# Gates and ids in a tensor of their own, two batches' parks on SyncE, eight copies on VectorE, and w2 behind w_out in a step

## The chip, the cores and the metric

The kernel runs on one core of a Trainium2 chip, so the execution has one slowest core and one clock. The metric is the device time of one execution in microseconds (us), the median of several runs. Five engines work at once and each runs its own instructions in order: TensorE (PE, matmuls; PEld is its weight loads), VectorE (DVE), ScalarE (ACT), GpSimd (POOL) and SyncE (SP, which here only issues DMAs). DMAs are issued from SP, from ACT and, where they are indirect, from POOL; a DMA instruction that has to wait holds whatever stands behind it on the engine that issues it.

## What is computed

Three layers in a row on 8 x 3072 tokens of 256 channels. First a long convolution along the sequence, written as an FFT. Then a mixture of 8 experts with one expert for each token, in which an expert takes at most 768 tokens *of the whole 24576*, in order; all others get a row of zeros. Last a dense pair of layers with a softplus between.

```python
# x: (8, 3072, 256)
X = np.fft.rfft(x, axis=1); y = np.fft.irfft(X * (filt_r + 1j * filt_i)[None], n=3072, axis=1)
x = y.reshape(24576, 256)
logits = x @ w_gate                         # (N, 8); e = argmax, gate = softmax at e
# token i goes to slot counts[e] of expert e as long as counts[e] < 768, in order of i
h = np.maximum(np.einsum('ecd,edf->ecf', disp, w1), 0.0)     # F = 1024
y = np.einsum('ecf,efd->ecd', h, w2)
out[i] = gate[i] * y[e, slot]               # 0 where the token has no slot
h2 = out @ w_in                             # (N, 2048)
return (np.maximum(h2, 0) + np.log1p(np.exp(-np.abs(h2)))) @ w_out
```

## The kernel before

**The convolution** is a DFT by two matmul stages each way (3072 = 96 x 32). Only the first three batches (called static, `STATIC = 3`) are convolved ahead, since they can fill all 6144 slots; more is computed only if a flag says that slots are empty. Of a batch, `tr1` transforms the input, `load_i` fetches a tile `it` of the half-way result from a DRAM tensor `mid`, `s2` multiplies it with `m2s` (L235) and with the filter (tile `z`), `s3` goes back (tile `e`), and then, for each of eight groups g of 384 rows and each half h of the channels, `tr2` transposes (L262) and copies to a tile `j` (L265), `s4` multiplies with `m4s` (L299) and copies to the tile `yt` (L300), and `park` (L365) writes `yt` to a DRAM tensor `parked` of the batch. `yt` has three buffers, and the zero tile `pf` with which `prefill` (L382) clears the dispatch tensor `disp` in 16 DMAs is one of them until the last of these DMAs has read it.

**The routing.** `gsum`, `gturn` and five steps of `gate` give each row its expert, its gate and its slot. `marks` writes gate and token id as two more columns into `parked` (256 floats of row and these 2, so a row has 258), in four DMAs of 8-byte pieces on SP (L372), and the slots into `slots` (L373). `send` loads the slots as an index (`ixt`, L390); `fetch` loads 384 parked rows with gate and id into a tile `lt` (L394; three buffers); `scatter` writes them to `disp` by indirect DMAs from POOL (L398), 24 for a batch. After the last scatter of batch 1 the first unit's rows `xd` are loaded (L535).

**Experts and dense layers** run over 16 units of 384 slots, two for each expert. `tr_x` turns `xd` to `xh`/`xl` (L555, L556), `w1` (L566) and `w2` (L583, tile `py`, taken to `yh`/`yl` by L589 and L590) are the expert; `wi` (L598, tile `pi`) the first dense layer, `sp_act` on ACT and `sp_sum` on DVE (L501, tile `g`) the softplus, `wo` (L621, tile `po`) the second. fp32 precision comes from products of high and low parts, so a weight `ws` is split into `w1h`, `w1l`, `w2h`, `w2l` by ACT and POOL (L412, L413); the dense weights come in as `wst` (L452) and are split by `convert` into `wih`, `wil`, `woh`, `wol` on DVE, ACT and POOL.

**What sets the order.** The program is emitted by hand: `ev(t, order, fn)` puts a piece of work at a step t with a rank, and the pieces are issued by step, then rank. The steps count from c0 = -72; below "step 20" is c0 + 20, and the steps from 0 on (72 after c0) are those in which `wi` and `wo` run. The batches begin at steps 0, 17 and 29. `marks` of a batch is 22 steps on, `send` 23; the prefills stand at steps 5 to 20, the four `wst` loads of `x_done` at 22, the scatters of batch 0 at 26 to 37 (two a step) and of batch 1 at 43 to 50 (three a step). The tail of the last static batch is at 44 to 52: two `tr2`, two `s4` and one park in each. From step 0 on the ranks say `w2`, `wi`, softplus, `wo`, and `w1` behind; `w2` is there in every other step, `w1` in the others.

DMAs from SP and ACT take turns, in the order in which they are written, on eight completion semaphores. A DMA therefore waits until the one eight places earlier has landed, from whichever of the two queues that was.

## Time and profile before

| what | us |
|---|---|
| median of 3 runs | 1128.05 |
| lowest and highest of them | 1123.34, 1129.77 |
| the profiled execution | 1124.01 |
| its span in the trace | 1122.1 |
| PE busy in the span | 1040.6 (93%) |
| ACT busy | 804.6 (72%) |
| POOL busy | 598.1 (53%) |
| DVE busy | 478.8 (43%) |

How to read it: the profiled execution is one execution and lies 4.04 us below the median and 0.67 us above the lowest run; 1.91 us of it lie outside the span. PE is the busiest engine over the whole, but the share is a mean over stages. The convolution lasts until about 262 us of the span and the way into the dense layers until about 365 us; behind that comes one long even stage. In the rows below, "a <- b" behind an engine says what it waited for: b is the releaser. In a timeline, the bracket says how long the engine was idle before the row, and on what.

### The profile page before, as it was taken

Reading aid. Unit: us, or ns where it says so; the run is one execution under the profiler, and the core shown is the slowest. Engines: PE = TensorE matmul, PEld = TensorE weight load, DVE = VectorE, ACT = ScalarE, POOL = GpSimd, SP = SyncE. Lnnn points to the kernel's source line nnn. Section 1 sums busy time; section 2 is a strip of 40 time slices with the busy share of each in tenths; the row PEclk is TensorE's granted clock in tenths of the full one; section 3 lists DMA queues with packets and bytes.
Section 4 is the critical chain, followed back from the end, with each engine's and each line's share of the span. In section 5 each row is a group of like instructions: output and inputs, shape, how many; then the busy total and the mean of one; then the engine's idle time right before and its main releaser. Section 6 shows DMA issues by size and latency. Waiting matters only on the chain.

```text
span 1122.1 us, 18349 instructions
## 1 busy us (share of the span) xinstructions
PE 1040.6 (93%) x6608; PEld 963.6 (86%) x6608; DVE 478.8 (43%) x929; ACT 804.6 (72%) x1690; POOL 598.1 (53%) x566
## 2 busy tenths in 40 slices
PE   9999788666778999999999999999999999999996
PEld 7655566336778999999999999999999999999996
DVE  3526699336867472323232333233333333232221
ACT  3554445455778888877887878888788787887885
POOL 0410284544555756677656564655646565554554
PEclk9999999977999999999999999999999999999999
DMA  9997787776542317633333333242211212100000
GB/s 305 319 323 207 191 247 164 210 239 148 159 130 83 91 48 254 217 109 129 113 114 113 109 113 114 91 144 81 76 53 55 60 52 62 53 11 15 15 15 18
DMA packets 111416, 141.69 MB, mean 126 GB/s; under 512 B 24367, under 2 KB 82988, under 8 KB 111313
## 3 DMA queue, kind: packets, MB, share of 16 engines
q1 hardware_dynamic: 87632, 105.73, 31.1%
q10 hardware_dynamic: 17920, 22.02, 6.8%
q0 software_dynamic: 5760, 12.65, 3.2%
q8 instruction: 54, 0.88, 0.3%
q14 instruction: 50, 0.40, 0.1%
HBM read 80.38 MB, written 63.15 MB: 128 GB/s over the span
## 4 chain that ended last, share of the span: by engine, by line
PE 71%; DMA 8%; DVE 6%; issue 6%; ACT 3%; POOL 3%; SPq 1%; POOLq 0%; ACTq 0%; DVEq 0%
PE pi L598 22%; PE po L621 22%; PE py L583 9%; PE pw L566 9%; DMA it<-mid 2%; DMA mid<-s 2%; PE p L235 2%; POOL disp L398 1%; PE p L199 1%; PE p L219 1%; PE p L299 1%; POOL gl L413 1%; PE p L254 1%; DVE wr L475 1%; DMA xt<-in_x_dram 1%
## 5 line engine op out<-in xcount | busy, mean ns | idle before, releaser
L501 DVE SCALAR_TENSOR_TENSOR g<-pi,ln 128x384 f32<-128x384 f32 x256 | 142.8, 558 | 498.5 <-ACT ln L496 455.5
L413 POOL TENSOR_TENSOR gl<-g,gh 128x384 fp32r<-128x384 f32 x256 | 260.5, 1021 | 114.4 <-ACT gh L412 76.3
L621 PE MATMUL po<-woh,gh 128*128 128x256 f32 x768 | 214.9, 280 | 3.7 <-DVE ot L628 3.7
L621 PE MATMUL po<-woh,gl 128*128 128x256 f32 x768 | 215.6, 281 | 0.8 <-POOL gl L413 0.8
L621 PE MATMUL po<-wol,gh 128*128 128x256 f32 x768 | 215.8, 281 | 0.0
L493 ACT ACTIVATE ab<-pi 128x384 f32<-128x384 f32 x256 | 125.0, 488 | 114.4 <-PE pi L598 103.3
L598 PE MATMUL pi<-yh,wih 128*128 128x384 f32 x512 | 173.5, 339 | 6.4 <-DVE g L501 6.4
L598 PE MATMUL pi<-yl,wih 128*128 128x384 f32 x512 | 172.4, 337 | 0.0
L598 PE MATMUL pi<-yh,wil 128*128 128x384 f32 x512 | 172.2, 336 | 0.0
L413 POOL TENSOR_TENSOR w1l<-ws,w1h 128x512 fp32r<-128x512 f32 x64 | 83.4, 1303 | 148.9 <-ACT w1h L412 145.4
L621 PEld LDWEIGHTS po<-woh,gh 128*128 128x128 f32 x768 | 144.3, 188 | 4.5 <-DVE ot L628 2.6
L621 PEld LDWEIGHTS po<-woh,gl 128*128 128x128 f32 x768 | 144.8, 188 | 1.0 <-POOL gl L413 1.0
L621 PEld LDWEIGHTS po<-wol,gh 128*128 128x128 f32 x768 | 144.2, 188 | 0.0
L494 ACT ACTIVATE ab<-ab 128x384 f32<-128x384 f32 (+1 forms) x257 | 134.9, 525 | 8.2
L496 ACT ACTIVATE ln<-ab 128x384 f32<-128x384 f32 (+1 forms) x257 | 134.8, 524 | 8.1
L412 ACT CAST gh<-g 128x384 fp32r<-128x384 f32 x256 | 129.6, 506 | 0.3 <-DVE g L501 0.3
L413 POOL TENSOR_TENSOR w2l<-ws,w2h 128x512 fp32r<-128x512 f32 x64 | 83.3, 1301 | 84.6 <-ACT w2h L412 82.7
L598 PEld LDWEIGHTS pi<-yh,wih 128*128 128x128 f32 x512 | 96.5, 188 | 8.5 <-DVE g L501 8.4
L243 POOL TENSOR_TENSOR z<-z,t 128x512 f32<-128x512 f32 x24 | 31.0, 1292 | 126.1 <-DVE t L242 94.9
L598 PEld LDWEIGHTS pi<-yl,wih 128*128 128x128 f32 x512 | 96.4, 188 | 0.0
L598 PEld LDWEIGHTS pi<-yh,wil 128*128 128x128 f32 x512 | 96.1, 188 | 0.0
L583 PE MATMUL py<-hh,w2h 128*128 128x384 f32 x256 | 89.6, 350 | 6.4 <-DVE yl L590 6.4
(132 smaller groups left out, 2000.7 us busy)
## 6 DMA issues: line engine op xcount, KB each, us to landing
ws<-in_w_dram SPq DMA_DIRECT2D x128, 256.0 KB
out_dram<-cs SPq DMA_DIRECT2D x48, 512.0 KB
lt<-parked SPq DMA_DIRECT2D x24, 387.0 KB
xt<-in_x_dram SPq DMA_DIRECT2D x24, 384.0 KB
parked<-yt ACTq DMA_DIRECT2D x24, 384.0 KB
disp<-pf SPq DMA_DIRECT2D x16, 387.0 KB
xd<-disp SPq DMA_DIRECT2D x48, 129.0 KB
mid<-s ACTq DMA_DIRECT2D x16, 384.0 KB
```

What stands on the lines that cost most here:

```text
L235: nc.tensor.matmul(ps[:, i], lhsT=self.m2s[:, p0 + i], rhs=it[:, i], start=True, stop=True)
L243: (nc.vector if b > 0 and k % 2 else nc.gpsimd).tensor_tensor(out=z, in0=z, in1=t2, op=ALU.add)
L412: nc.scalar.copy(dst_hi, src)
L413: nc.gpsimd.tensor_tensor(out=dst_lo, in0=src, in1=dst_hi.bitcast(F32), op=ALU.subtract)
L493: nc.scalar.activation(out=ab[:, :n], in_=h, func=ACTF.Abs)
L494: nc.scalar.activation(out=ab[:, :n], in_=ab[:, :n], func=ACTF.Exp, scale=-1.0)
L496: nc.scalar.activation(out=ln[:, :n], in_=ab[:, :n], func=ACTF.Ln, bias=1.0)
L501: nc.vector.scalar_tensor_tensor(out=g[:, :n], in0=h, scalar=0.0, in1=ln[:, :n], op0=ALU.max, op1=ALU.add)
L566: nc.tensor.matmul(ps, lhsT=a[:, k, fs], rhs=b[:, k], start=(n == 0), stop=(n == 5))
L583: nc.tensor.matmul(self.py[d], lhsT=a[:, j % 2, ds], rhs=b, start=(j == 0 and n == 0), stop=(j == 7 and n == 2))
L598: nc.tensor.matmul(self.pi, lhsT=a[i][:, k], rhs=b[:, k], start=(n == 0), stop=(n == 5))
L621: nc.tensor.matmul(self.po[t], lhsT=a[:, ts], rhs=b[:, i], start=(i == 0 and n == 0), stop=(i == KI - 1 and n == 2))
```

## The change

It does five things. **Tensors:** `parked` keeps 256 columns, and gates and ids go to a new DRAM tensor `marked` of two columns. A park then writes 96 contiguous pieces of 4 KB where it wrote 384 of 1 KB; `marks` is one DMA instead of four; `load_rows` is two DMAs, one for the rows and one for gate and id, whose pieces in the tile are 8 bytes. **Queues:** the parks of batches 0 and 1 are issued by SP, those of batch 2 stay on ACT. **Copies:** of the last batch, the copies to `j` with h = 0, eight in all, go to DVE. **Steps:** the prefills come three steps later, `marks` one, `send` with its two fetches two, the scatters of batch 0 one. **Ranks:** `w2` comes behind `wi`, the softplus and `wo` in a step. Behind the change the lines of the file move by one or two: L365 is L367, L394 is L395 and L396, L452 is L454, L583 is L585, L598 is L600.

```diff
@@ -112,7 +112,8 @@
     const = ctx.enter_context(tc.tile_pool(name="const", bufs=1))
     dram = ctx.enter_context(tc.tile_pool(name="dram", bufs=1, space=DRAM))
     disp = dram.tile([nslot, D + 2], F32, name="disp")
-    parked = [dram.tile([S, D + 2], F32, name=f"parked{b}") for b in range(STATIC)]
+    parked = [dram.tile([S, D], F32, name=f"parked{b}") for b in range(STATIC)]
+    marked = [dram.tile([S, 2], F32, name=f"marked{b}") for b in range(STATIC)]
     slots = [dram.tile([S], I32, name=f"slots{b}") for b in range(STATIC)]
     mid = [dram.tile([N1 * N2, D], F32, name=f"mid{b}") for b in range(1, STATIC)]
     ltp = ctx.enter_context(tc.tile_pool(name="lt", bufs=3))
@@ -262,7 +263,7 @@
                 nc.tensor.transpose(ps[:, i], self.e[b][:, h, :, 4 * g + i], ident)
             pv = ps.rearrange("p a c -> p (a c)")
             self.jt[b, h, g] = self.jp.tile([N1, 512], F32, name="j", tag="j")
-            nc.scalar.copy(self.jt[b, h, g], pv)
+            (nc.vector.tensor_copy if b == STATIC - 1 and h == 0 else nc.scalar.copy)(self.jt[b, h, g], pv)
 
         def gsum(self, b):
 
@@ -293,11 +294,12 @@
         def s4(self, b, h, g):
             cs = slice(h * 128, h * 128 + 128)
             if h == 0:
-                self.yt[b, g] = self.yp.tile([N1, 4, D + 2], F32, name="yt", tag="yt")
+                yt = self.yp.tile([N1, 4 * (D + 2)], F32, name="yt", tag="yt")
+                self.yt[b, g] = yt[:, 0:4 * D]
             jt = self.jt.pop((b, h, g))
             ps = pso.tile([N1, 4, 128], F32, name="p6", tag="o")
             nc.tensor.matmul(ps.rearrange("p a c -> p (a c)"), lhsT=self.m4s, rhs=jt, start=True, stop=True)
-            nc.scalar.copy(self.yt[b, g][:, :, cs], ps)
+            nc.scalar.copy(self.yt[b, g].rearrange("p (a c) -> p a c", c=D)[:, :, cs], ps)
 
         def gate(self, b, late):
 
@@ -361,20 +363,19 @@
 
         def park(self, b, g):
 
-            rows = parked[b].rearrange("(g n a) c -> n g a c", n=N1, a=4)[:, g, :, 0:D]
-            nc.scalar.dma_start(rows, self.yt[b, g][:, :, 0:D])
+            queue = nc.scalar if b == STATIC - 1 else nc.sync
+            queue.dma_start(parked[b].rearrange("(g n a) c -> g n (a c)", n=N1, a=4)[g], self.yt[b, g])
 
         def marks(self, b):
 
             ga, ix = self.route[b]
-            rows = parked[b].rearrange("(g n a) c -> n g a c", n=N1, a=4)
-            for a in range(4):
-                nc.sync.dma_start(rows[:, :, a, D:D + 2], ga.rearrange("n (g a) o -> n g a o", a=4)[:, :, a])
+            nc.sync.dma_start(marked[b].rearrange("(g n a) o -> n g (a o)", n=N1, a=4),
+                              ga.rearrange("n (g a) o -> n g (a o)", a=4))
             nc.sync.dma_start(slots[b].rearrange("(g n a) -> n g a", n=N1, a=4), ix.rearrange("n (g a) -> n g a", a=4))
 
         def prefill(self):
 
-            pf = self.yp.tile([N1, 4, D + 2], F32, name="pf", tag="yt")
+            pf = self.yp.tile([N1, 4 * (D + 2)], F32, name="pf", tag="yt").rearrange("p (r c) -> p r c", c=D + 2)
             nc.gpsimd.memset(pf, 0.0)
             nc.gpsimd.memset(pf.bitcast(I32)[:, :, D + 1:D + 2], OOB)
             dv = disp.rearrange("(a p r) c -> a p r c", p=N1, r=4)
@@ -391,7 +392,8 @@
 
     def load_rows(b, g):
         rows[b, g] = ltp.tile([128, 3, D + 2], F32, name="lt", tag="lt")
-        nc.sync.dma_start(rows[b, g], parked[b].rearrange("(g p t) c -> g p t c", p=128, t=3)[g])
+        nc.sync.dma_start(rows[b, g][:, :, 0:D], parked[b].rearrange("(g p t) c -> g p t c", p=128, t=3)[g])
+        nc.sync.dma_start(rows[b, g][:, :, D:D + 2], marked[b].rearrange("(g p t) o -> g p t o", p=128, t=3)[g])
 
     def scatter_rows(b, g, t, group):
         n = hi if group == "late" else nslot
@@ -735,7 +737,7 @@
                 fn(*args)
 
         units = [Unit(e, r + e * UNIT) for r in [hi, *range(0, hi, region)] for e in range(E)]
-        W2, WI, SP, WO, SUM, W1, TAKE, TR, AHEAD = range(9)
+        WI, SP, WO, W2, SUM, W1, TAKE, TR, AHEAD = range(9)
         T1, T2, S2, GG, S4, GATE, S3, X1, ON = range(-9, 0)
 
 
@@ -844,20 +846,20 @@
                 ev(t + 1, S4, cv.s4, b, h, g)
                 if h:
                     ev(t + 1, ON, park, b, g)
-            ev(s + 22, ON, cv.marks, b)
+            ev(s + 23, ON, cv.marks, b)
             if not last:
-                ev(s + 23, ON, send, b, "lead")
+                ev(s + 25, ON, send, b, "lead")
                 for _ in range(2):
-                    ev(s + 23, ON, fetch)
+                    ev(s + 25, ON, fetch)
         for g in range(8):
             ev(c0 + 5 + g, X1, cv.x1_out, 1, g)
             ev(c0 + 5 + g, ON, cv.load_x, 2, g)
             ev(c0 + 13 + g, X1, cv.x1_out, 2, g)
         for i in range(nslot // (4 * N1)):
-            ev(c0 + 5 + i, ON, next, fills)
-        for t in range(26, 51):
-            if t < 38 or t > 42:
-                ev(c0 + t, ON, scatter, 2 if t < 38 else 3)
+            ev(c0 + 8 + i, ON, next, fills)
+        for t in range(27, 51):
+            if t < 39 or t > 42:
+                ev(c0 + t, ON, scatter, 2 if t < 39 else 3)
         ev(c0 + 22, ON, x_done)
         for t in range(c0 + 23, -24):
             ev(t, AHEAD - 0.5, convert, t < c0 + 45 and (t - c0) % 3 == 2)
```

On SP, this is the place where batch 0's marks stood, before: the marks and the slots, then the four `wst` loads of `x_done`, the index, and the first loads of rows. (`parked_61` and `slots_64` are those of batch 0.)

```order
L382 DMA disp<-pf 96x1032 x9
L372 DMA parked_61<-ga 96x8x2 x4
L373 DMA slots_64<-ix 96x8x4
L452 DMA wst<-in_win_dram 128x2x128 x4
L390 DMA ixt<-slots_64 128x8x3
L394 DMA lt<-parked_61 128x774 x3
L452 DMA wst<-in_win_dram 128x2x128
L394 DMA lt<-parked_61 128x774 x2
```

After, the parks of batch 0 stand between the prefills, and the `wst` loads ahead of the marks:

```order
L367 DMA parked_61<-yt 96x1024
L383 DMA disp<-pf 96x1032 x2
L454 DMA wst<-in_win_dram 128x2x128 x4
L367 DMA parked_61<-yt 96x1024
L372 DMA marked_64<-ga 96x8x8
L374 DMA slots_67<-ix 96x8x4
L383 DMA disp<-pf 96x1032
L367 DMA parked_61<-yt 96x1024
L391 DMA ixt<-slots_67 128x8x3
L395 DMA lt<-parked_61 128x3x256
L396 DMA lt<-marked_64 128x3x2
L395 DMA lt<-parked_61 128x3x256
```

The four `wst` loads moved from behind the marks to before them, and six parks now stand ahead of the index load, one of them behind the marks.

On ACT, this is the tail of the last batch, before, from the second half of step 44 to the split of the first expert weight (`parked_63` is batch 2, `parked_62` batch 1):

```order
L365 DMA parked_62<-yt 384x1x256
L365 DMA parked_63<-yt 384x1x256
L480 ACTIVATE whb<-wtop,ebias 128x256
L481 ACTIVATE wrf<-wrf 128x256
L300 COPY yt<-p_2019 96x4x128
L300 COPY yt<-p_2022 96x4x128
L265 COPY j<-p_2025 96x512
L265 COPY j<-p_2032 96x512
L314 ACTIVATE ex<-dl 96x256
L365 DMA parked_63<-yt 384x1x256
L300 COPY yt<-p_2111 96x4x128
```

After, from the same place:

```order
L367 DMA parked_63<-yt 96x1024
L482 ACTIVATE whb<-wtop,ebias 128x256
L483 ACTIVATE wrf<-wrf 128x256
L302 COPY yt<-p_2029 96x4x128
L302 COPY yt<-p_2032 96x4x128
L266 COPY j<-p_2042 96x512
L316 ACTIVATE ex<-dl 96x256
L367 DMA parked_63<-yt 96x1024
L302 COPY yt<-p_2122 96x4x128
L302 COPY yt<-p_2125 96x4x128
L266 COPY j<-p_2135 96x512
L367 DMA parked_63<-yt 96x1024
```

One park is gone from ACT (batch 1's last), one copy to `j` of each pair is gone, and the parks of batch 2 keep their places.

On PE, this is the beginning of step 0, before: `w2` of the third unit's first piece and then `wi` of the first unit:

```order
L583 MATMUL py<-hh,w2h 128x384
L583 MATMUL py<-hl,w2h 128x384
L583 MATMUL py<-hh,w2l 128x384
L583 MATMUL py<-hh,w2h 128x384
L583 MATMUL py<-hl,w2h 128x384
L583 MATMUL py<-hh,w2l 128x384
L598 MATMUL pi<-yh,wih_1023 128x384
L598 MATMUL pi<-yl,wih_1023 128x384
L598 MATMUL pi<-yh,wil_1031 128x384
L598 MATMUL pi<-yh,wih_1023 128x384
L598 MATMUL pi<-yl,wih_1023 128x384
L598 MATMUL pi<-yh,wil_1031 128x384
```

After, at the same place:

```order
L600 MATMUL pi<-yh,wih_1020 128x384
L600 MATMUL pi<-yl,wih_1020 128x384
L600 MATMUL pi<-yh,wil_1028 128x384
L600 MATMUL pi<-yh,wih_1020 128x384
L600 MATMUL pi<-yl,wih_1020 128x384
L600 MATMUL pi<-yh,wil_1028 128x384
L585 MATMUL py<-hh,w2h 128x384
L585 MATMUL py<-hl,w2h 128x384
L585 MATMUL py<-hh,w2l 128x384
L585 MATMUL py<-hh,w2h 128x384
L585 MATMUL py<-hl,w2h 128x384
L585 MATMUL py<-hh,w2l 128x384
```

The six matmuls to `pi` moved ahead of the six to `py`; in the following steps `wi` therefore stands alternately behind a `w2` and behind a `w1`, where before the two stood together behind `wi` of every second step.

## Rows read from the trace of the kernel before

**Rows 1.** Stretches: length, busy us (instructions) of each engine, granted clock, DMA share, GB/s.

```profile
0.00:89.00 89.00, 82.49 (x470) 58.10 (x471) 34.19 (x54) 42.57 (x73) 16.43 (x18) 1.00 0.99 314
89.00:136.00 47.00, 39.05 (x178) 25.58 (x177) 32.07 (x58) 20.59 (x39) 6.37 (x5) 0.93 0.72 188
136.00:200.00 64.00, 54.51 (x338) 40.40 (x340) 60.20 (x107) 34.09 (x68) 39.42 (x38) 1.00 0.79 205
200.00:262.30 62.30, 36.84 (x156) 18.77 (x156) 18.06 (x44) 27.13 (x55) 30.99 (x31) 0.79 0.75 205
262.30:315.00 52.70, 41.34 (x220) 38.84 (x220) 48.41 (x102) 37.17 (x89) 31.16 (x29) 0.95 0.58 174
315.00:365.00 50.00, 44.31 (x266) 42.23 (x267) 34.63 (x71) 41.85 (x98) 27.64 (x28) 0.97 0.33 93
365.00:1122.10 757.10, 742.07 (x4990) 739.67 (x4989) 251.25 (x495) 601.20 (x1271) 446.14 (x419) 1.00 0.26 86
```

**Rows 2.** What PE waited for, 100 to 136 us: us in total, times, longest.

```profile
PE p L235 <- DMA it<-mid: 6.6, 3, 3.5
```

**Rows 3.** The chain that ended last, 105 to 132 us: start, us, what.

```profile
105.55 0.69 DVE z L239
...
114.87 7.76 DMA wst<-in_win_dram
122.66 8.65 DMA it<-mid
```

**Rows 4.** Timeline of SP, DMA issues in order: start, us, engine, line.

```profile
66.87 15.63 SPq L382 DMA_DIRECT2D disp<-pf  x9
111.55 2.06 SPq L372 DMA_DIRECT2D parked<-ga  x4
```

**Rows 5.** Copies and parks in the whole trace: ns shortest/median/longest, first and last start.

```profile
L365 ACTq DMA_DIRECT2D parked<-yt x24: 557/558/1890, 83.6 to 261.2; - x24
...
L265 ACT COPY j<-p x48: 580/584/615, 76.2 to 248.1; 96x512 f32<-96x512 f32 x48
```

**Rows 6.** What PE waited for, 200 to 290 us, as in Rows 2.

```profile
PE p L299 <- ACT j L265: 8.0, 4, 6.1
PE p L299 <- DVE v L317: 6.4, 1, 6.4
PE pt L555 <- ACT xd L547: 6.0, 2, 4.8
PE pw L566 <- ACT xh L556: 5.1, 1, 5.1
```

**Rows 7.** Timeline of ACT in the last tail; bracket: idle before, and on what.

```profile
218.25 1.24 ACTq L365 DMA_DIRECT2D parked<-yt  x2
...
230.46 0.59 ACTq L365 DMA_DIRECT2D parked<-yt  x1
231.15 1.07 ACT L300 COPY yt<-p 96x512 f32<-96x512 f32 x2 [8.57 <-DMA ws<-in_w_dram]
...
238.94 0.62 ACT L412 CAST w1h<-ws 128x512 fp32r<-128x512 f32 x1
```

**Rows 8.** The chain again, 196 to 261 us.

```profile
196.13 6.76 DMA lt<-parked
...
248.79 2.55 DMA disp<-lt,ixt
...
253.92 7.18 DMA parked<-ga
```

**Rows 9.** What PE waited for, 290 to 380 us, as in Rows 2.

```profile
PE py L583 <- DVE yl L590: 6.4, 2, 3.9
PE pi L598 <- DVE g L501: 5.4, 6, 1.5
```

**Rows 10.** Scatters in the whole trace (as in Rows 5), and what their tile made wait.

```profile
L398 POOL DMA_INDIRECT disp<-lt,ixt x72: 967/992/1447, 136.3 to 548.9; - x72
...
  DMA lt<-parked: 8.6, 1
```

## The prediction

> **What bounds the kernel now.** I read the stretches first, then what TensorE waited for in each, then the chain, then the timelines of the engines that the chain names. The stretches [rows 1] fall into two kinds. From 365 us on TensorE is busy for 742.07 of 757.1 us; nothing in this change makes its matmuls fewer, so at most a few us are to be had there. Ahead of 365 us it is idle for 66.5 us of 365 (the lengths less the busy times of the first six rows), and 25.5 of these lie in 200 to 262.3, where the granted clock is 0.79 as well; 8.0 lie in 89 to 136. In 136 to 200 and in 262.3 to 315 VectorE is the busy one (60.20 of 64, 48.41 of 52.7), in 315 to 365 ScalarE (41.85 of 50). So a saving counts where TensorE waits on something that is neither of these.
>
> Two places are of that kind. **The first** is at 111 us: the waits of TensorE are 6.6 us in three pieces on tiles fetched from DRAM [rows 2], and the chain [rows 3] and SP's timeline [rows 4] say why: the marks of batch 0 go out at 111.55, behind the routing's last VectorE work, the weight loads stand behind them on SP and take 7.76 us, and only when the load's semaphore is free can the next `it` load go, which takes 8.65 more. SP is done with the prefills at 82.50 (66.87 + 15.63) and issues nothing until 111.55 [rows 4]: 29 us behind one wait. **The second** is the last tail. TensorE waits 8.0 on copies `j`, 6.4 on VectorE's `v`, 6.0 on `xd` and 5.1 on `xh` [rows 6], 25.5 us in all. ScalarE's rows [rows 7] show that it is held by its own DMAs: two parks go out only at 218.25, one at 230.46, behind which ScalarE was idle 8.57 us on an expert weight load. The chain [rows 8] then goes through the last scatter (248.79) and the marks of batch 2 (253.92, 7.18 us), which the last park waits for on ScalarE with `xh` behind it.
>
> **The early part: marks, loads, parks on SP.** Removed: SP's hold ahead of the weight loads. In the order after, the four `wst` loads stand before the marks, with one park and two prefills just ahead. The `it` loads then no longer depend on marks. Of the 6.6 us I expect 5.0 back, and about 1 us more of a smaller wait earlier as the prefills leave the stretch whose DMA share is 0.99: **6 us**. The upper bound is 8.0, all of the idle time in 89 to 136 [rows 1]. The lower bound is 2: the weight loads now start behind transfers of 384 KB, and one such round trip is as long as the `it` load's, 8.65 us, so most of the wait may come back. Moving 16 parks from ScalarE frees 16 x 0.558 = 8.9 us of its queue [rows 5], but ScalarE is busy 34.09 of 64 in 136 to 200, with VectorE full there; I cost that at nothing either way. SP has room, except for what the slower rival below says. A park of 96 pieces in place of 384 moves the same bytes; I take no gain from it, and if the DMA share of 0.72 to 0.79 falls, it helps loads that are already counted. Batch 0's scatters are a step later and end well before those of batch 1 begin: nothing.
>
> By the Trainium skill, page "Trainium Kernel Development and Optimization", section Key Constraints, DMAs of SP, ScalarE and GpSimd share the same 16 engines, and issuing from several queues only saves issue time. That rule alone would make the sixteen parks worth at most the 8.9 us above; the rows show a second effect, since what holds ScalarE for 8.57 us is the wait before an issue and no issue.
>
> **The last tail.** Eight `j` copies leave ScalarE: 8 x 0.584 = 4.7 us [rows 5] of work that lies one per step between a pair of transposes and its matmul. No VectorE copy of this shape is in the trace; the nearest, `z` of 128x512 from the same kind of source, takes 0.69 us [rows 3], so 8 x 0.69 = 5.5 us on an engine busy 18.06 of 62.3. The two copies of a pair then run beside each other. What the ScalarE queue waits for moves as well. By the semaphores that the order gives each DMA, the parks of batch 2 now wait as follows: the first on an early weight load (no hold), the next on the fourth pair of row loads, which follows the sixth scatter, the third on the fifth, the fourth on the fourth expert weight load, and the last on nothing but its copies. With scatters and loads where they are now, the first goes out by about 213 in place of 218.25, the second near 220 (rows landed at 202.9 [rows 8], six scatters of about 1.3 with what lies between them to near 211, where one alone is 0.99 [rows 10]; the landing of a scatter, 2.55, and a load of 6.76 [rows 8]) in place of 230.46, the fourth near 230, and so `w1h`, at 238.94 now [rows 7], at 230 to 234: 5 to 9 us. The scatters that stand behind its low part on GpSimd, the `xd` loads and TensorE's first expert matmul follow. On top, the last park no longer waits for the marks (7.18 us landing, of which `xh` and TensorE lose 5.1 [rows 6, 8]). Both lie on the one chain, 5 and 5: **10 us**. Lower bound 4: the first half is taken back by the loads' landing, and part of the last 5.1 goes to `xd` or a weight split that is late next. Upper bound 13: 9 and 4 at full clock instead of 0.79. What follows in 262.3 to 315 is bound by VectorE's splits, in order and behind the same work, so I let it shift as a whole.
>
> **w2 behind w_out.** In step 0 `py` must wait until the former `py` is taken: 6.4 us over two waits, the longest 3.9 [rows 9]. In the order after, `wi` of a unit whose input is long there runs in that wait; six matmuls, at 742.07 us for 4990 [rows 1], fill 0.9 us of it. Its softplus starts earlier by that wait, and `wi` comes evenly afterwards, against waits of 5.4 us on `g`; ScalarE's 41.85 of 50 lets only some of that go. I take **2 us**, with bounds of -2 (the copies `yh` now stand behind three softplus operations on ScalarE) and 5. Behind 365 us the 15 us that TensorE isn't busy are spread thin: 0.
>
> **The sum.** 6 + 10 + 2 = 18 us from the profiled 1124.01: 1106.0 on its basis. The median lies 4.04 above it and the lowest run 0.67 below, so the basis of the timed runs is 0 to 4 higher; I take 2 and say **1108**. The bounds: 2 + 4 - 2 = 4 gives 1120 and 8 + 13 + 5 = 26 gives 1098; with 0 to 4 for the basis, 1098 to 1124.
>
> **Rivals.** *(a) The small loads become the clock.* Each row load now has a twin of 8-byte pieces, 24 more DMAs. The nearest row for such pieces is the marks' landing, 7.18; the load of rows is 6.76 [rows 8], so beside it the twin costs 0 to 0.4 us, but up to 7 more for each turn of three buffers if the two land one after the other. Two parks wait for such a pair. Then `w1h` stays near 237, the tail gains 4 instead of 10, and the sum is 12 less 2 for batch 1's later start: 10, 1116. For it: two parks do wait on row loads; against it: of 72 scatters one waited for rows, the first of batch 1 [rows 10].
> By the Trainium skill, page "DMA: Bandwidth & Descriptors", section Specifications, transfers below 512 bytes don't run at line rate and are read, changed and written. By that rule the twins are the dear part of this change, and (a) would be the likelier; the rows of the same small pieces, which land in about the time of the 387 KB load, speak against more than that.
>
> *(b) Everything goes and the clock stays up.* All waits of rows 2, 6 and 9 fall to their bounds and 200 to 262.3 runs nearer to clock 1: 26 us, 1100 or a little less.
>
> *(c) Given back.* The two places open, but VectorE, full in 136 to 200 and 262.3 to 315, is behind the same work and lets nothing of the early part through, and the tail's gain is waited for at the splits: 18 becomes 4 or less, 1122 to 1126, within 0.5%.
>
> *(d) Slower: the ring of `yt`.* It has three buffers, and with the prefills three steps later one of these is `pf` until step 23; so ScalarE's copies of a group wait until the park two groups back has landed. These parks now stand on SP behind prefills, each 1.7 us of SP in a row of nine [rows 4]. Two groups are 3.25 steps, about 16 us (all parks, steps 16 to 52, go out from 83.6 to 261.2 [rows 5], 4.9 us a step). A landing is 7 to 9 us [rows 3, 8], so it decides once a park waits over 7 to 9 us on SP. If it does, three groups before step 23 lose a round trip of 8.65 each, 26, and the early 6 is gone: 26 lost, 12 saved behind it, 1140. Against it: the order has a park behind one or two prefills at most.
>
> **How the numbers follow.** The forecast 0.55 (1101 to 1114), (a) 0.15, (b) 0.08, (c) 0.12, (d) 0.10. Half a percent, about what a measurement of this kernel can tell, is 5.6 us: faster is below 1122.4, slower above 1133.7. Faster: the forecast, (a) and (b), 0.78; same: (c) and a little of (a) and (d), 0.14; slower 0.08. The range leaves out (d), the far end of (b) and that of (c): 1097 to 1124.
>
> **What would show it.** Right: no wait of TensorE on `it` over 2 us between 100 and 136; SP issues weight loads before the marks; no park on ScalarE later than about 232 until the last; `xh` without a wait on marks; `pi` runs inside the wait on `py`. Wrong: ScalarE's `yt` copies waiting for `parked` between 85 and 115 (d); GpSimd waiting for `lt` more than once between 196 and 225 (a); the stretch to 315 as long as before although 200 to 262 is shorter (c). If ScalarE still waits for a weight load in the tail, my reading of which DMA each park waits for is wrong.

## The result, and the profile after

The changed kernel takes 1114.67 us, median of 8 runs (1111.69 to 1117.72), against 1123.46 of the kernel before in 8 runs (1121.35 to 1129.77). The medians differ by 8.8 us; the ratio, which compares all runs of both, is 0.9914, with an interval of 0.989 to 0.9938: 0.86%, or 9.7 us, faster. The forecast was 1108, 16 us below the 1124 of the profiled execution; the measured time lies in its range, and a little over half of the gain came. Its profile has a span of 1112.5 us, 9.6 less than before. Where the 9.6 lie is not where the prediction put them.

The stretches of the changed kernel, with the columns and borders of [rows 1]:

```profile
89.00:136.00 47.00, 43.17 (x227) 30.42 (x225) 41.29 (x71) 25.87 (x50) 12.86 (x11) 1.00 0.94 277
...
200.00:262.30 62.30, 46.18 (x195) 31.34 (x193) 42.97 (x93) 34.99 (x78) 38.08 (x37) 0.86 0.78 234
...
365.00:1112.50 747.50, 727.49 (x4838) 718.02 (x4837) 242.37 (x475) 591.60 (x1228) 429.50 (x402) 1.00 0.26 85
```

Fixed borders mix what moved with what shrank: 200 to 262.3 has 46.18 us of TensorE where it had 36.84 and a granted clock of 0.86 in place of 0.79, but it no longer holds the same work. Four events that stand in both programs cut the span by work instead: the marks of batch 1 on SP, the first expert matmul, the first copy of `ot`, and the last.

| start, us | before | after | earlier by |
|---|---|---|---|
| marks of batch 1 (SP) | 186.70 | 178.56 | 8.1 |
| first expert matmul, to `pw` (PE) | 262.32 | 239.53 | 22.8 |
| first copy `ot` (DVE) | 384.94 | 361.21 | 23.7 |
| last group of copies `ot` | 1111.97 | 1102.31 | 9.7 |

The front gained 23.7 us and the even stage behind it gave 14.1 back. TensorE's waits in the even stage, of before and then of after (as in [rows 2]: us in total, times, longest):

```profile
PE po L621 <- DVE ot L628: 3.7, 3, 2.4
PE pi L598 <- DVE g L501: 1.0, 1, 1.0
PE po L621 <- POOL gl L413: 0.8, 1, 0.8
```

```profile
PE po L623 <- ACT ab L495: 6.6, 12, 0.5
PE po L623 <- DVE ot L630: 2.7, 4, 1.2
PE pi L600 <- DVE g L503: 1.2, 1, 1.2
```

Twelve waits of 0.5 us are new, about one for each unit. The copies `ot` show the pace: in ten of the fifteen intervals between units they came 51.1 us apart before, and come 52.3 to 52.4 apart now. One unit of before, and one of after (columns of [rows 1]):

```profile
646.38:697.49 51.11, 51.11 (x344) 51.05 (x343) 16.36 (x36) 41.07 (x87) 29.12 (x28) 1.00 0.33 109
```

```profile
627.08:679.45 52.37, 51.82 (x343) 51.14 (x342) 16.48 (x35) 41.91 (x87) 29.26 (x28) 1.00 0.33 111
```

Before, TensorE is busy without a gap; after, a unit takes 1.26 us more, of which 0.55 show as idle time. The place is at the beginning of a unit, where `wo` needs the buffers of `po` back. VectorE there in the changed kernel, and TensorE (timelines; the bracket is idle time before, and its releaser):

```profile
626.60 0.56 DVE L573 SCALAR_TENSOR_TENSOR hl<-pw,hh 128x384 fp32r<-128x384 f32 x1 [0.36 <-ACT hh L572]
627.08 1.08 DVE L630 COPY ot<-po 128x256 f32<-128x256 f32 x3
```

```profile
626.76 0.34 PE L600 MATMUL pi<-yh,wil 128*128 128x384 f32 x1
627.64 0.35 PE L623 MATMUL po<-woh,gh 128*128 128x256 f32 x1 [0.55 <-ACT ab L495]
```

The first matmul to `po` starts 0.88 us after the last to `pi`; it can start when the first `ot` is copied out of its buffer, and the copies stand on VectorE behind `hl`, the split of `w1`'s result, which waits for ScalarE's `hh` (idle 0.36 us on it in the row above) and so for `w1` itself. The releaser's name in TensorE's row, `ab`, is the event that came last by the profile, not the one waited for: its row starts at 627.13 and lasts 0.49, so it ends within 0.12 us of the first of the three copies. A run below tells the two apart. Between two units' `wo` there stood `w1`, `w2` and `wi` before; now `w1` and `wi` do.

In the front, the waits that answer to [rows 2] and [rows 6], 100 to 136 us and 200 to 290:

```profile
PE p L236 <- DMA it<-mid: 1.7, 2, 1.3
```

```profile
PE p L301 <- DVE j L266: 6.2, 5, 4.7
PE pt L557 <- ACT xd L549: 4.0, 4, 1.9
PE p L301 <- ACT j L266: 3.2, 2, 1.8
...
PE pw L568 <- ACT xh L558: 0.7, 1, 0.7
```

6.6 became 1.7, and the 5.1 on `xh` became 0.7. Of the 8.0 on ScalarE's copies `j` 3.2 are left, with 6.2 on VectorE's beside them; the 6.4 on `v` are gone, and the 6.0 on `xd` are 4.0. (The second window has fixed borders, so it doesn't hold the same work.) ScalarE's parks and the first split in the last tail (answering to [rows 7]):

```profile
213.64 0.31 ACTq L367 DMA_DIRECT2D parked<-yt  x1
...
218.66 0.31 ACTq L367 DMA_DIRECT2D parked<-yt  x1
219.01 0.62 ACT L414 CAST w1h<-ws 128x512 fp32r<-128x512 f32 x1 [3.17 <-DMA ws<-in_w_dram]
...
238.65 0.31 ACTq L367 DMA_DIRECT2D parked<-yt  x1
```

Of the chain, the parts that answer to [rows 8]:

```profile
187.35 4.38 DMA lt<-marked
...
208.09 5.47 DMA lt<-parked
```

The split `w1h` starts at 219.01, 19.9 us earlier than before, and the last park, at 238.65, waits for no marks. Last, the first step of the dense layers (answering to [rows 9]):

```profile
PE pi L600 <- DVE g L503: 5.1, 4, 2.6
PE py L585 <- DVE yl L592: 2.9, 1, 2.9
```

### The profile page after: what moved, and what is told of

Same layout as the page of the kernel before. It is cut to its first block, busy times and chain, and to the rows that moved or that the text cites. A ratio compares the mean times of both kernels' runs of the same rounds, so it can differ in the third digit from the quotient of the medians.

```text
span 1112.5 us, 18383 instructions
## 1 busy us (share of the span) xinstructions
PE 1048.5 (94%) x6608; PEld 966.5 (87%) x6608; DVE 486.3 (44%) x937; ACT 810.7 (73%) x1682; POOL 599.8 (54%) x566
## 4 chain that ended last, share of the span: by engine, by line
PE 72%; DVE 10%; DMA 6%; ACT 5%; issue 4%; POOL 2%; ACTq 1%; SPq 0%; POOLq 0%; DVEq 0%
PE pi L600 22%; PE po L623 22%; PE py L585 10%; PE pw L568 9%; PE p L220 2%; PE p L200 1%; PE p L236 1%; DMA disp<-lt,ixt 1%; ACT ab L495 1%; DVE wr L477 1%; POOL gl L415 1%; DVE whb L485 1%; DVE wrf L479 1%; DVE t L241 1%; DVE t L243 1%
## 5 line engine op out<-in xcount | busy, mean ns | idle before, releaser
L600 PE MATMUL pi<-yh,wih 128*128 128x384 f32 x512 | 176.2, 344 | 6.3 <-DVE g L503 6.3
L600 PE MATMUL pi<-yh,wil 128*128 128x384 f32 x512 | 173.2, 338 | 0.0
L600 PE MATMUL pi<-yl,wih 128*128 128x384 f32 x512 | 172.6, 337 | 0.0
L623 PEld LDWEIGHTS po<-woh,gh 128*128 128x128 f32 x768 | 145.0, 189 | 14.6 <-ACT ab L495 12.8
L600 PEld LDWEIGHTS pi<-yh,wih 128*128 128x128 f32 x512 | 96.6, 189 | 11.4 <-DVE g L503 10.4
L572 ACT ACTIVATE hh<-pw 128x384 fp32r<-128x384 f32 x128 | 62.6, 489 | 56.1 <-PE pw L568 56.1
L600 PEld LDWEIGHTS pi<-yl,wih 128*128 128x128 f32 x512 | 96.6, 189 | 0.0
L600 PEld LDWEIGHTS pi<-yh,wil 128*128 128x128 f32 x512 | 96.3, 188 | 0.0
L585 PE MATMUL py<-hh,w2h 128*128 128x384 f32 x256 | 87.9, 343 | 5.5 <-DVE yl L592 5.5
```

The costliest lines, as they stand in the source:

```text
L572: nc.scalar.activation(out=hh, in_=ps, func=ACTF.Relu)
L585: nc.tensor.matmul(self.py[d], lhsT=a[:, j % 2, ds], rhs=b, start=(j == 0 and n == 0), stop=(j == 7 and n == 2))
L600: nc.tensor.matmul(self.pi, lhsT=a[i][:, k], rhs=b[:, k], start=(n == 0), stop=(n == 5))
L623: nc.tensor.matmul(self.po[t], lhsT=a[:, ts], rhs=b[:, i], start=(i == 0 and n == 0), stop=(i == KI - 1 and n == 2))
```

## The experiments

Each run has its ratio to the kernel before on the same chip; that is what is compared, since the chips' own medians of before went from 1123 to 1129. The trace of each gives the four events of the table above. The last four rows belong to the runs at the end of this section.

| kernel | ratio (95% interval) | median, us | marks, batch 1 | first `pw` | first `ot` | last `ot` | unit |
|---|---|---|---|---|---|---|---|
| the changed kernel | 0.9914 (0.989 to 0.9938) | 1114.67 | 178.56 | 239.53 | 361.21 | 1102.31 | 52.4 |
| old ranks | 0.9769 (0.9733 to 0.9804) | 1103.5 | 177.43 | 241.73 | 365.34 | 1093.24 | 51.1 |
| ranks alone | 1.011 (1.0068 to 1.0151) | 1141.75 | 191.08 | 265.65 | 386.89 | 1129.89 | 52.3 |
| take first | 0.9792 (0.9753 to 0.9831) | 1107.49 | 178.12 | 240.86 | 363.15 | 1097.07 | 51.6 |
| old ranks, no copies on VectorE | 0.9753 (0.9715 to 0.9791) | 1101.94 | 178.33 | 238.46 | 362.75 | 1089.76 | 51.1 |
| old ranks, parks on ScalarE | 0.9892 (0.9852 to 0.9931) | 1117.05 | 185.95 | 248.41 | 372.12 | 1099.86 | 51.1 |
| old ranks, marks in the rows | 0.9868 (0.9828 to 0.9909) | 1114.84 | 183.37 | 253.35 | 376.37 | 1103.47 | 51.1 |
| old ranks, old steps | 0.9746 (0.9693 to 0.9799) | 1100.89 | 177.82 | 241.31 | 364.67 | 1092.45 | 51.1 |
| the tensor alone | 0.9899 (0.9859 to 0.994) | 1116.62 | 184.09 | 252.08 | 376.11 | 1103.15 | 51.1 |
| old ranks, pieces of 1 KB | 0.9851 (0.9818 to 0.9885) | 1105.2 | 177.77 | 243.17 | 365.78 | 1092.85 | 51.1 |
| old ranks, again | 0.9789 (0.9764 to 0.9813) | 1106.05 | 179.17 | 242.96 | 367.29 | 1094.28 | 51.1 |
| pieces of 1 KB, again | 0.9809 (0.9787 to 0.983) | 1107.65 | 184.55 | 250.99 | 375.24 | 1102.26 | 51.1 |
| what shows a gain, together | 0.9738 (0.9698 to 0.9777) | 1091.24 | 172.01 | 230.85 | 350.82 | 1077.93 | 51.1 |

Two repeats show how far these numbers carry. One program gave 0.9769 and 0.9789 on two chips, another 0.9851 and 0.9809, so 0.2 to 0.4 points (2 to 5 us) between chips are no difference yet. And each row of events is one execution: the marks of batch 1 stand at 177.77 and 184.55 in two executions of one program, and at 186.70 and 191.08 in the kernel before and in the run of its ranks alone, whose order is the same up to step 0. The units agree within 0.1 us from run to run, the events of the front only within several us.

**The ranks.** The first two runs take the new ranks away from the changed kernel, and put nothing but them into the one before.

```diff
-        WI, SP, WO, W2, SUM, W1, TAKE, TR, AHEAD = range(9)
+        W2, WI, SP, WO, SUM, W1, TAKE, TR, AHEAD = range(9)
```

> The changed kernel with the ranks of before (w2 ahead of wi in a step); all else as changed. Theory A (the new ranks lengthen each unit of the even stage by 52.36 - 51.10 = 1.26 us, over the eleven units from the second to the thirteenth first copy of `ot`, about 13 us): units of 51.1 again, first copy of `ot` at about 362 (1 us later than 361.2), span about 1100, time about 1102. Rival B (the even stage is longer because the earlier start brings something else with it, such as expert weights that come no earlier, or the queue of SP with twice the loads): units stay at 52.4 and the time at 1114.

> The kernel before with nothing but the new ranks. Theory A: units of 52.4 in place of 51.1, first copy of `ot` 0 to 2 us earlier, time 1123.5 + 13 - 1 = about 1135. Rival B: units of 51.1 and a time of 1121 to 1123, the 2 us that the prediction gave the ranks.

With the old ranks the units are 51.1 again and the ratio is 0.9769, 1.45 points below the changed kernel's. The ranks alone make the kernel before 1.1% slower, 12.6 us of its 1129.12, with units of 52.3. Theory A stands, and rival B falls twice. From the first `pw` to the first `ot` the way is 122.6 us before and 121.2 with the ranks alone, 123.6 with the old ranks and 121.7 in the changed kernel: in the front, the ranks do give 1.4 to 1.9 us. (In the ten traces with the old order this way takes 122.6 to 124.3.)

**Why the units got longer.** One more rank moves:

```diff
-        WI, SP, WO, W2, SUM, W1, TAKE, TR, AHEAD = range(9)
+        WI, SP, WO, W2, SUM, TAKE, W1, TR, AHEAD = range(9)
```

> The changed kernel with one more change of rank: the copies out of `po` (take) ahead of w1 in a step, so that on VectorE they no longer stand behind the split of w1's result. In the changed trace TensorE loses 0.78 us of a unit between the last matmul to `pi` and the first to `po`, and 2 x 0.46 behind the transposes (0.28 each before). Theory A1 (`po` comes free late because its copy stands behind the split `hl`, which waits for ScalarE and w1): the 0.78 goes, units of about 51.6, time about 1106. Rival A2 (the first matmul to `po` waits for `gh` or `gl` of ScalarE and GpSimd, as the releaser's name says): units stay at 52.4, time 1114.

VectorE at the beginning of a unit, and TensorE's waits over ten units:

```profile
627.42 1.08 DVE L630 COPY ot<-po 128x256 f32<-128x256 f32 x3
628.42 0.55 DVE L573 SCALAR_TENSOR_TENSOR hl<-pw,hh 128x384 fp32r<-128x384 f32 x1
```

```profile
PE po L623 <- DVE ot L630: 2.2, 2, 1.4
```

The copies now stand ahead of `hl`, the twelve waits are gone, and a unit takes 51.6. So A1 holds: it was the copies out of `po`, queued behind the split of a `w1`, and not `gh` or `gl`. About 0.5 us a unit is left of the 1.26; of this, 0.36 fits the gap behind the transposes (0.46 lost twice in a unit against 0.28 twice before), which is as long in this run as in the changed kernel. No run took that away.

**The copies on VectorE.** All copies to `j` back on ScalarE, with the old ranks:

```diff
-            (nc.vector.tensor_copy if b == STATIC - 1 and h == 0 else nc.scalar.copy)(self.jt[b, h, g], pv)
+            nc.scalar.copy(self.jt[b, h, g], pv)
```

> As the run with the old ranks, but all copies to `j` on ScalarE as before. If the eight copies on VectorE carry a large part of what the last tail gained beyond the forecast (first expert matmul 22.8 us earlier, of which 8.1 were there at batch 1's marks): 4 to 8 us above the run with the old ranks. If the tail's gain is that of the waits on DMAs alone: within 2 us of it, since ScalarE had 30 us of idle time in 62 us there.

The ratio is 0.9753 against 0.9769: no difference, if anything a gain. TensorE's waits between 200 and 290 us with the copies on both engines, and (180 to 245 us) on ScalarE alone:

```profile
PE p L301 <- DVE j L266: 10.2, 3, 4.9
```

```profile
PE pt L557 <- ACT xd L549: 6.7, 2, 6.3
PE p L301 <- ACT j L266: 5.4, 2, 5.0
```

On VectorE the copies stand behind the routing, and TensorE waits 10.2 us for them; without them it waits 5.4 for ScalarE's, and then longer for `xd`. From the marks of batch 1 to the first `pw` it takes 64.3 us with the copies on both engines and 60.1 on ScalarE alone, and 61.0 in the changed kernel: there is no gain of the copies to be seen.

**The queue, the tensor and the steps**, each undone alone, with the old ranks. First the queue:

```diff
-            queue = nc.scalar if b == STATIC - 1 else nc.sync
+            queue = nc.scalar
```

> As the run with the old ranks, but the parks of batches 0 and 1 on ScalarE as before. Theory P (SP as the queue is worth the issue time only, hidden in the early part, and what counts is that marks have a tensor of their own and come later): within 4 us of the run with the old ranks, ratio to before 0.975 to 0.981. Rival Q (a park that waits for a semaphore holds ScalarE, and the move takes that away): 8 us or more above it, ratio 0.984 or more, with the loss in the stretch up to the marks of batch 1 (177.4 there, 186.7 before) and in the tail.

Then the tensor:

```diff
-    parked = [dram.tile([S, D], F32, name=f"parked{b}") for b in range(STATIC)]
-    marked = [dram.tile([S, 2], F32, name=f"marked{b}") for b in range(STATIC)]
+    parked = [dram.tile([S, D + 2], F32, name=f"parked{b}") for b in range(STATIC)]
...
-            nc.sync.dma_start(marked[b].rearrange("(g n a) o -> n g (a o)", n=N1, a=4),
-                              ga.rearrange("n (g a) o -> n g (a o)", a=4))
...
+            for a in range(4):
+                nc.sync.dma_start(rows[:, :, a, D:D + 2], ga.rearrange("n (g a) o -> n g a o", a=4)[:, :, a])
...
```

> As the run with the old ranks, but gates and ids as columns of the parked rows again: four DMAs for a batch's marks, parks of 384 pieces of 1 KB, one load for rows with gate and id. Theory P: the marks' DMAs stand again between parks and loads of one tensor; the last park waits for the marks with xh behind it (5.1 us of TensorE before), and the marks' landing is 7 us instead of 3 to 4: 7 to 12 us above the run with the old ranks, ratio 0.983 to 0.988. Rival (the twin loads cost what the separate tensor saves): within 3 us of it, ratio at most 0.980.

And the steps:

```diff
-            ev(s + 23, ON, cv.marks, b)
+            ev(s + 22, ON, cv.marks, b)
...
-                ev(s + 25, ON, send, b, "lead")
+                ev(s + 23, ON, send, b, "lead")
...
-            ev(c0 + 8 + i, ON, next, fills)
+            ev(c0 + 5 + i, ON, next, fills)
...
```

> As the run with the old ranks, but the steps of prefills, marks, sends and scatters as before. If the loads of weights gain by standing ahead of the marks (step 22 and 23): first weight load of x_done at about 114 in place of 106.6, the 6 to 8 us of the early part gone, ratio about 0.983. If the queue and the tensor alone open the early part, the loads no longer wait long: within 2 us, ratio 0.977.

With the parks on ScalarE the ratio goes up by 1.0 to 1.2 points, 12 to 14 us, though the seven runs spread from 1108.79 to 1123.14 (by the intervals it is some 6 to 20): the size is that of rival Q. The loss is where it was expected first, ahead of batch 1's marks (185.95 against 177.43 and 179.17, with 186.70 before), and not in the tail: from the marks to the first `pw` it takes 62.5 us, with the parks on SP 64.3. By 136 us TensorE has done 647 matmul instructions, as in the kernel before (646), where both runs with the old ranks have done 696. TensorE's wait for `it` is back, with the parks on ScalarE (75 to 190 us) and then on SP (75 to 180 us):

```profile
PE p L236 <- DMA it<-mid: 8.8, 5, 4.9
```

```profile
PE p L236 <- DMA it<-mid: 2.7, 3, 1.5
```

Whether this is rival Q's cause is not shown. The move does a second thing, which no expectation names: on SP the parks, which wait there for ScalarE's copies `yt`, stand between the prefills and spread them. SP with the parks on ScalarE, a part of the chain of that run, and SP with the parks on SP:

```profile
68.57 18.04 SPq L383 DMA_DIRECT2D disp<-pf  x11
112.83 3.06 SPq L454 DMA_DIRECT2D wst<-in_win_dram  x4
```

```profile
80.54 12.04 DMA it<-mid
```

```profile
68.21 5.32 SPq L383 DMA_DIRECT2D disp<-pf  x4
...
106.58 6.27 SPq L454 DMA_DIRECT2D wst<-in_win_dram  x4
```

Without the parks eleven prefills go out in a row (nine in the kernel before [rows 4]), and an `it` load behind them takes 12.04 us. No run spreads the prefills with the parks on ScalarE, so the two causes stand side by side.

With gates and ids in the rows the loss is 0.8 to 1.0 points, 9 to 11 us, as theory P had it: in the two traces 5.9 ahead of batch 1's marks and 5.7 from there to the first `pw`. ScalarE in that run shows what the prediction's slower rival described, its `yt` copies waiting for buffers that a park or the last prefill holds (75 to 200 us); SP stands at the four DMAs of the marks for 5.54 us, where the changed kernel's one takes 0.34:

```profile
ACT yt L301 <- DMA disp<-pf: 4.8, 1, 4.8
...
ACT yt L301 <- DMA parked<-yt: 3.9, 2, 2.8
```

```profile
112.22 0.56 SPq L366 DMA_DIRECT2D parked<-yt  x1
113.05 5.54 SPq L374 DMA_DIRECT2D parked<-ga  x4
```

The steps are worth nothing (0.9746 against 0.9769). The first weight load of `x_done` then starts at 112.86, behind the marks as before, and the early gain is there all the same: marks of batch 1 at 177.82.

**The tensor alone**, put into the kernel before: `marked` as in the change, with

```diff
...
-            nc.scalar.dma_start(rows, self.yt[b, g][:, :, 0:D])
+            queue = nc.scalar
+            queue.dma_start(parked[b].rearrange("(g n a) c -> g n (a c)", n=N1, a=4)[g], self.yt[b, g])
```

> The kernel before with the new tensor alone: gates and ids apart, one DMA for marks, parks of 96 pieces of 4 KB, two loads for rows; parks on ScalarE, all copies on ScalarE, steps and ranks of before. By the prediction's own terms: the marks' wait of the last park goes (5 us) and the early part and ScalarE's holds stay: about 5 to 7 us faster than before, ratio 0.994 to 0.996. Rival: the shorter marks and loads already give most of it, ratio below 0.987; or the twins cost it, ratio 1.0 or more.

0.9899, between the two expectations: 11 to 12 us of 1128.71. Of these, in the two traces, 2.6 lie ahead of batch 1's marks and 7.6 from there to the first `pw`; the wait of `xh` on the marks is gone, and ScalarE's holds in the tail got shorter too, though its parks stayed (`w1h` starts 48.3 us behind the marks, where it was 52.2).

**The size of the pieces.** The tensor's rows kept 258 columns wide with two unused, so that parks are 384 pieces of 1 KB, but the marks stay apart (old ranks; the parks and loads follow).

```diff
-    parked = [dram.tile([S, D], F32, name=f"parked{b}") for b in range(STATIC)]
+    parked = [dram.tile([S, D + 2], F32, name=f"parked{b}") for b in range(STATIC)]
```

> As the run with the old ranks, with gates and ids in a tensor of their own, but the parked rows 258 columns wide with two unused: parks of 384 pieces of 1 KB again, and loads of three such pieces. If the tensor's 11 us (run with the marks in the rows against the run with the old ranks) come from the marks no longer standing between parks and loads of one tensor: within 3 us of the run with the old ranks, ratio 0.974 to 0.980. If they come from the larger pieces: 7 us or more above it, ratio 0.983 or more.

> The run with the old ranks once more, beside the one with pieces of 1 KB on the same chip, since the ratios of those two (0.9769, 0.9851) came from different chips and their profiled spans (1102.9, 1102.2) say the opposite. If the pieces are worth the 9 us of the ratios: this run is 7 to 11 us below the other.

> The run with pieces of 1 KB once more, beside the one with the old ranks. If the spans are right and the pieces are worth nothing: within 2.5 us of that run.

The first such run gave 0.9851 (0.9818 to 0.9885) on another chip than the run with the old ranks: by the ratio it falls on the side of the larger pieces, by its time (1.7 us above) on that of the marks. On one chip the two take 1106.05 and 1107.65 us, ratios 0.9789 (0.9764 to 0.9813) and 0.9809 (0.9787 to 0.983): 1.6 us by the medians, 2.3 by the ratios. A gain of the larger pieces is not shown, and one of up to some 6 us is not excluded. The marks and loads are the likelier source of the tensor's gain; but the run with the marks in the rows, whose pieces are of 1 KB too, lies only 0.2 to 0.6 points above these two, so how the gain divides is open.

**What shows a gain, put together.** The tensor and the parks on SP; steps and copies of before; and `w2` behind `wo` in steps 0 to 5 alone.

```diff
-                ev(b + 2 * j if v > 1 else 8 * v - 16 + j, W2, u.w2, j)
+                t = b + 2 * j if v > 1 else 8 * v - 16 + j
+                ev(t, WO + 0.5 if 0 <= t < 6 else W2, u.w2, j)
```

> Only what has shown a gain: the tensor and the parks on SP; steps and copies as before, and the new rank of w2 in steps 0 to 5 alone, the old one afterwards. If the parts add up: units of 51.1, the way from the first expert matmul to the first copy of `ot` about 122 us (123.6 with the old ranks, 121.7 with the new), time 1099 to 1101, ratio 0.973 to 0.975. If steps and copies matter together though neither does alone: 1104 or more.

1091.24 us against 1123.13 on that chip, a ratio of 0.9738 (0.9698 to 0.9777): faster than both kernels of this case. By its ratio it is no better than the run without copies on VectorE (0.9753), so the ranks of the first steps are not shown to matter in time. From the first `pw` (230.85) to the first `ot` (350.82) it takes 120.0 us, where the traces with the old order take 122.6 to 124.3.

## Why the prediction was right, and where it was not

The time lies in the range and on the side forecast, but by two errors that cancel in part: a front that gained 23.7 us where the sum had 18, and an even stage that gave 14.1 back where it had 0. That they cancel is luck.

**Early part, 6 us (2 to 8).** Marks of batch 1 came 8.1 us earlier: the upper bound, and its size is as good as right. The mechanism was wrong. The prediction let the gain come from the weight loads' place ahead of the marks; with the old steps they stand behind them again and the gain stays. It costed the sixteen parks that leave ScalarE at "nothing either way", and that is the step that failed: with these back on ScalarE, where the `it` loads are issued too, the marks come at 185.95 and 12 to 14 us of the time are lost. The new tensor has a part in it as well: without it they come at 183.37, with it alone at 184.09. How much of the early part is whose is not shown, since two executions of one program lie 6.8 us apart there.

By the Trainium skill, page "Trainium Kernel Development and Optimization", section Key Constraints, issuing from several queues saves issue time only. By that rule alone the sixteen parks were worth 8.9 us at most with the issues of before, and 5.2 in the run that puts them back, where one takes 0.33 us (both estimates). The runs show 12 to 14 us, and some 6 at the lower end of the intervals, so they lie above the rule's value for that run; whether by what waiting issues held up or by the spread of the prefills is open.

**Last tail, 10 us (4 to 13).** From the marks of batch 1 to the first expert matmul 75.6 us became 61.0: 14.6 us, above the bound. Which park waits for what was read right, as far as the trace shows it: the third goes out at 213.64, when a load of rows has landed, the fourth at 218.66, behind ScalarE's wait of 3.2 us for an expert weight. (The prediction's own sign against this reading, a wait for a weight load in the tail, contradicts its list, in which the fourth park waits for one.) What was mis-sized is `w1h`: 19.9 us earlier, or 11.8 beyond the early part's 8.1, where 5 to 9 were said. Of these, 3.0 lie ahead of the first scatter, which the prediction left where it was: from marks to the first rows of batch 1 it took 16.2 us before (186.70 to 202.89) and takes 13.2 now (178.56 to 191.73, the landing of its first marked load). The rest was not taken apart further, and traces with the same order up to the first `pw` differ by 3.3 us here (61.0 to 64.3). `xh`'s wait fell by 4.4, as forecast. The eight copies on VectorE, 4.7 us of ScalarE's work in the prediction, show no gain.

**262 to 315 shifts as a whole.** It did: from the first `pw` to the first `ot` 122.6 us became 121.7. Rival (c), given back to VectorE, is out.

**w2 behind w_out, 2 us (-2 to 5).** In step 0 the wait for `py` fell from 3.9 to 2.9, about the 0.9 that was said, and the waits of `pi` from 5.4 to 5.1 only; 0.9 us in the front as a whole. With the even stage the ranks cost some 13 us, far outside the bounds of -2 to 5. The step that failed is "Behind 365 us [...] 0". The even stage has one place per unit where TensorE needs its buffers back from VectorE, and in the old order twelve matmuls of `w2` and `wi` hid that; the price is 1.26 us in most units and 14.1 in all. The row was to be had beforehand: the order of VectorE's instructions at the end of a unit, `hl` ahead of `ot`, together with the six matmuls that would be left to cover it.

The sum as measured: 8.1 + 14.6 + 0.9 - 14.1 = 9.5 of 9.6.

**The rivals.** (a), the small loads as the clock, did not come, though its sign did: between 196 and 225 us GpSimd waits three times for a marked load, 2.7 us in all. From 185 to 260 us it is five scatters and 11.8 us, but 8.1 of these are the first one's, which waited 8.6 before [rows 10]:

```profile
POOL disp L400 <- DMA lt<-marked: 11.8, 5, 8.1
```

(d), the ring of `yt`, is there with 1.9 us in one wait, and grows to 8.7 us only where the marks hold SP, in the run with the marks in the rows. (b), everything goes, is about what comes out without the ranks' price: with the old ranks the ratio is 0.9769 to 0.9789, 24 to 26 us. Its clock did not come: 200 to 262.3 us runs at 0.86 in the changed kernel, where it was 0.79.

## What to carry to other kernels

A change of order that fills one wait has to be costed in every place where that order repeats: look for what stood between the last use of a buffer and its next on the engine that waits, and for what stands ahead of the release on the engine that releases (here 1 to 2 us at the head were paid for with about 1.26 us in each of eleven units). Moving a DMA issue to another queue can be worth more or less than its issue time (here 12 to 14 us against 5.2): look at what waits ahead of it on either queue, and at what that wait holds back or spreads behind it. Data that are written late can belong in a tensor apart from those written early; that was worth 9 to 12 us here. When a forecast comes true, cut both spans at the same events before believing its reasons.

## What the runs showed of the hardware that was not expected

Loads in pieces of 8 bytes landed as fast as large ones. The 24 marked loads of the changed kernel and their time from issue to landing (shortest/median/longest), and then the 24 loads of rows in the same trace:

```profile
L396 SPq DMA_DIRECT2D lt<-marked x24: 523/620/1967, 123.6 to 466.4; - x24
...
DMA to landing us min/median/max: 3.4/4.4/7.0
```

```profile
L395 SPq DMA_DIRECT2D lt<-parked x24: 517/524/958, 122.9 to 465.9; - x24
...
DMA to landing us min/median/max: 4.0/5.2/7.8
```

Their median is 4.4 us, that of the loads of rows 5.2. By the Trainium skill, page "DMA: Bandwidth & Descriptors", section Specifications, transfers below 512 bytes fall behind line rate; at 384 such pieces a load, beside the rows' load, what could show it are the 3.7 us of scatters' waits above (11.8 less 8.1).

Pieces of 4 KB against 1 KB showed no difference in time beyond the noise (1.6 us between the two runs on one chip, whose intervals overlap), but one in issue: on ScalarE a park of 96 pieces takes 0.31 us in the changed kernel, one of 384 pieces 0.56 [rows 5], and 0.56 again in the run with pieces of 1 KB.
